# A head's values at a pitch of 80 columns instead of 65 in a chunked attention and feed-forward kernel

## The chip, the cores and the metric

The kernel runs on one core of one Trainium2 chip. The core has five engines that run their own instruction streams: TensorE (PE, matrix multiplications, with weight loads beside it: PEld), VectorE (DVE), ScalarE (ACT), GpSimd (POOL) and SyncE (SP). Sixteen DMA engines move data between the device's memory and the on-chip memory; here GpSimd issues every load that casts from 32-bit to 16-bit floats (queue q0, software_dynamic) and SyncE issues all others (queue q1, hardware_dynamic). The metric is the device time of one execution in microseconds (us), the median of five runs.

## The reference

Four batches, eight heads, 768 positions, 64 values to a head. Positions are cut into chunks of 32. A chunk attends to eight memory keys of its head and to the keys from 16 positions ahead of the chunk to 8 behind it. The heads' outputs, side by side (512 wide), go through a layer norm and a feed-forward of width 2048 with a residual:

```
for each chunk c:
    k_full = concat(mem_k, k[l_start:r_end]);  v_full = concat(mem_v, v[l_start:r_end])
    a      = softmax(q[chunk] @ k_full.T / 8)
    x[chunk] = a @ v_full
xn  = (x - mean(x)) / sqrt(var(x) + 1e-6) * g_ln
out = x + relu(xn @ w_ch1) @ w_ch2
```

All inputs and the output are 32-bit floats; the kernel multiplies in 16-bit.

## The kernel before, in words

A *tile* is 128 positions; there are 24, six to a batch. A *unit* is three tiles, and the main loop at the end of the kernel walks over eight units. In unit u TensorE does the feed-forward of that unit's three tiles: sixteen steps of `up` (each 128 of the 2048 hidden columns, L319, followed by a ReLU on VectorE for even steps, L327, on ScalarE for odd ones, L325), then twelve steps of `down` (L336). Between the steps a plan written by hand places the attention work of the next unit's tiles: `scores` (L238), exponentials on ScalarE (L245), `values` (L258), `norm` on VectorE (L268 to L278), `turn_x` (L296), and the preparation of keys and queries for a later batch (`kq_block`: turns on TensorE at L176, copies on VectorE at L191 and on ScalarE at L201). The order of each engine's work is the order in which the program is written; each engine waits only for the data and buffers that it needs. Two pairs of PSUM buffers (`att`) serve attention and the turns, four single ones (`mm`) the feed-forward.

Weights for the whole feed-forward stay on chip (`w1c0` to `w1c3`, `w2c0` to `w2c3`). They are loaded once, by GpSimd, in the same queue as the first batch's keys, queries and values. In the order of issue: four loads of keys and queries, value groups 0 to 3, groups 4 and 5, `w1c0` to `w1c2`, the rest of keys and queries, `w1c3`, `w2c0`, `w2c1`, value groups 6 and 7, `w2c2`, groups 8 to 11, `w2c3`. Eight semaphores go round for these loads, so the ninth load after another is issued only when that one has landed.

Before the loop, a start is written out by hand: turns of the first keys and queries, `scores` and `values` of tiles 0 to 2, with multiplications of a zero tile between them (`stay_busy`, L310) that only keep TensorE occupied. `values` of tile t needs the value groups 2t and 2t+1.

The buffer that the change touches is `V` (two of them, one to a batch in turn): 128 rows, then 12 groups of 64 positions, then 8 heads, then `HD` columns of 16-bit floats. Rows 0 to 7 hold the memory values, rows 8 to 95 the positions around a group. Of a head's columns the first 64 are the values and the next one is 1.0, so that the matmul at L258 gives the sum of the exponentials as its 65th column. Who writes `V`:

- `clear_v` (L376 to L386, VectorE): zeros in the rows that fall outside the sequence (L378, L379), ones in column 64 of groups 1 to 10 (L380), and a copy of a 0/1 column into column 64 of groups 0 and 11 (L383). It is called once in the start for `V0` and once in unit 0, at step 8, for `V1`.
- `load_v_group` (L114): one group, up to 88 rows by 8 heads, 64 values each. Batches 0 and 1 are loaded so.
- `load_v_head` (L120): one head, 64 rows by 12 groups. Batches 2 and 3 are loaded so, and `v_around` (L128, L129, SyncE) then copies the overlapping rows from group to group.
- `v_mem` (L133, SyncE): the memory values, from `memv16`, which has the same columns.

Of the kernel before, what the change touches and what calls it, by code (L numbers as in the profile page):

```python
# [15 lines left out]
def kernel(  # L16
# [12 lines left out]
    nc = tc.nc  # L29
# [3 lines left out]
    NG = 12  # L33
    KR = 96
    KC = NG * KR + 32
    HD = 65
    CUT = 64

    ctx.enter_context(tc.manual_schedule())
# [5 lines left out]
    memk16 = sb.tile([128, 2, 64], FP16, name="memk16")  # L45
    memv16 = sb.tile([72, B, H, HD], FP16, name="memv16")[64:72, :, :, :]
    memv32 = sb.tile([72, 512], FP32, name="memv32")[64:72, :]
# [12 lines left out]
    q16 = [sb.tile([96, H, 8, 64], FP16, name=f"q16_{i}") for i in range(2)]  # L60
    V = [sb.tile([128, NG, H, HD], FP16, name=f"V{i}") for i in range(2)]
    KT = [sb.tile([128, 4, KC], FP16, name=f"KT{i}") for i in range(2)]
# [19 lines left out]
    def slot(kind):  # L82
        lst = {"att": att, "mm": mm}[kind]
        turn[kind] = (turn[kind] + 1) % len(lst)
        return lst[turn[kind]]

    def dram(t, offset, pattern):
        return bass.AP(tensor=t.tensor, offset=offset, ap=[list(p) for p in pattern])

    def free(ap, off, pattern, parts=None):  # L90

        p = list(ap.ap[0]) if parts is None else [ap.ap[0][0], parts]
        return bass.AP(tensor=ap.tensor, offset=ap.offset + off, ap=[p] + [list(x) for x in pattern])
# [37 lines left out]
    def v_mem(b):  # L131
# [3 lines left out]
            in_=bass.AP(tensor=src.tensor, offset=src.offset,  # L135
                        ap=[list(src.ap[0]), [0, NG], [1, H * HD]]),
        )
# [115 lines left out]
    def values(b, t):  # L253
        p = summed[t] = slot("att")
        for h in range(H):
            for gg in range(2):
                c0 = 128 * (h % 4)
                nc.tensor.matmul(  # L258
                    out=p[64 * gg : 64 * gg + 64, h // 4, c0 : c0 + HD],
                    lhsT=AT[t % 3][0:KR, gg, h, :],  # L260
                    rhs=V[b % 2][0:KR, 2 * t + gg, h, :],
                    start=(h % 4 == 0), stop=(h % 4 == 3), tile_position=(0, 64 * gg),
                )

# [111 lines left out]
    def clear_v(i, between=lambda: None):  # L376

        nc.vector.memset(V[i][0:32, 0, :, 0:64], 0.0)  # L378
        nc.vector.memset(V[i][64:96, NG - 1, :, 0:64], 0.0)  # L379
        nc.vector.memset(V[i][:, 1 : NG - 1, :, 64:65], 1.0)  # L380
        between()
        for c, g in enumerate((0, NG - 1)):
            nc.vector.tensor_copy(  # L383
                out=free(V[i][:, g, 0, 64:65], 0, [[HD, H]]),
                in_=free(counts[:, c : c + 1], 0, [[0, H]]),
            )  # L386
# [10 lines left out]
    nc.vector.memset(busy, 0.0)  # L397
    nc.vector.memset(counts, 1.0)
    nc.vector.memset(ones32, 1.0)
    nc.vector.memset(memv16[:, :, :, 64:65], 1.0)  # L400
    nc.sync.dma_start(out=memk32, in_=dram(mem_k, 0, [[64, 128], [128 * 64, 2], [1, 64]]))
    nc.sync.dma_start(out=g_one, in_=dram(moe_g_ln, 0, [[0, 1], [1, 512]]))
    nc.sync.dma_start(out=memv32, in_=dram(mem_v, 0, [[64, 8], [512, H], [1, 64]]))
# [7 lines left out]
    nc.scalar.copy(out=memv16[:, 0, :, 0:64], in_=memv32.rearrange("p (h d) -> p h d", h=H))  # L411
    stay_busy(10)
    clear_v(0, lambda: clear_q(0, 0))
    clear_q(0, 1)
    clear_k(0)
# [28 lines left out]
    for g in range(8, NG):  # L444
# [3 lines left out]
        out=memv16[:, 1:B, :, 0:64],  # L448
# [31 lines left out]
    scores(0, 1)  # L480
    stay_busy(5)
    values(0, 0)
    norm(0, 0)
    scores(0, 2)
    stay_busy(1)
    values(0, 1)
    norm(1, 1)
    stay_busy(4)
    values(0, 2)
    norm(2, 2)  # L490
    stay_busy(2)
# [11 lines left out]
    for u, tiles in enumerate(units):  # L503
# [18 lines left out]
        if u == 0:  # L522
            at(1, clear_q, 1, 0)
            at(5, clear_q, 1, 1)
            at(8, clear_v, 1)
            at(11, clear_k, 1)
            for j in (0, 2):
# [19 lines left out]
        elif u in (2, 4):  # L547
            attend(((1, 8, 8, 12), (4, 8, 10, 14), (11, 17, 17, 21)))
            b = u // 2 + 1
# [13 lines left out]
        for step in range(16 + 4 * n):  # L563
            if step < 16:
                up(u, n, step)
            else:
                i, part = divmod(step - 16, 4)
                if u == 0:
                    d = step - 16
                    i, part = divmod(d, 2) if d < 6 else (d % 3, d // 3)  # L570
# [36 lines left out]
```

The softmax here doesn't subtract the row's maximum and nothing guards it: scores larger than these inputs give would overflow.

## Time and profile before

| what | value |
|---|---|
| median of five runs | 232.03 us (231.02 to 233.15) |
| the profiled execution: its time, its span | 231.44 us, 229.7 us |
| PE busy | 222.7 us (97%) |
| DVE, ACT, POOL busy | 125.5 us (55%), 119.0 us (52%), 68.5 us (30%) |
| DMA queue q0 (GpSimd's loads) | 45680 packets, 14.23 MB |
| DMA queue q1 (SyncE's) | 4602 packets, 7.33 MB |
| value loads, `load_v_group` | 24, of which 20 with 88 KB each, 13.2 us from issue to landing (median) |
| value loads, `load_v_head` | 16, 96 KB each, 5.4 us |
| granted TensorE clock | 9 tenths or more in every slice |

Busy time is the sum over an engine's instructions; the KB of a load are those that it writes. A DMA share over 1 in a window means that more packets are under way on the sixteen engines than one each. The GB/s of a window count the bytes as written: a load that casts reads twice as many.

### The profile page before, as it was taken

How to read it: one execution, taken by the hardware profiler on the slowest of the kernel's cores; microseconds unless marked ns; L12 is line 12 of the kernel's file. 1: busy time of each engine (PE TensorE's matmuls, PEld its weight loads, DVE VectorE, ACT ScalarE, POOL GpSimd, SP SyncE). 2: the span in 40 equal slices, each digit the busy share in tenths (PEclk: the TensorE clock that was granted, in tenths of full speed). 3: DMA queues.
4: the chain of work that ended last, by engine and by line, in shares of the span. 5: the costliest groups of instructions: out<-in, count | busy, mean ns of one | idle time of the engine just before them, and what ended most of it. 6: DMA issues, size and time to landing. Idle time of an engine off the chain costs nothing.

```text
span 229.7 us, 5499 instructions
## 1 busy us (share of the span) xinstructions
PE 222.7 (97%) x2289; PEld 138.3 (60%) x2289; DVE 125.5 (55%) x290; ACT 119.0 (52%) x228; POOL 68.5 (30%) x125
## 2 busy tenths in 40 slices
PE   7988999999999999999999999999999999999993
PEld 2554676547765577555765577556764576556553
DVE  5756781565737638575436548674436542663222
ACT  3674648353893576655356367654456345534200
POOL 6974344677360370540001360410001200030000
PEclk9999999999999999999999999999999999999999
DMA  5999999999999999548921199553001200111012
GB/s 76 176 88 202 205 211 152 143 202 229 105 74 157 202 135 29 37 85 122 236 38 49 60 115 24 37 101 104 0 3 46 91 3 0 47 49 46 0 49 93
DMA packets 50307, 21.91 MB, mean 95 GB/s; under 512 B 37817, under 2 KB 46777, under 8 KB 50234
## 3 DMA queue, kind: packets, MB, share of 16 engines
q0 software_dynamic: 45680, 14.23, 89.1%
q1 hardware_dynamic: 4602, 7.33, 10.5%
q8 instruction: 18, 0.29, 0.6%
q14 instruction: 7, 0.06, 0.1%
HBM read 28.48 MB, written 6.29 MB: 151 GB/s over the span
## 4 chain that ended last, share of the span: by engine, by line
PE 77%; DMA 16%; POOL 2%; DVE 2%; issue 1%; POOLq 0%
PE mm L319 32%; PE mm L336 32%; DMA w2c<-in_moe_w_ch_dram 13%; PE att L238 4%; DMA V<-in_v_dram 4%; PE att L258 3%; PE att L176 3%; PE att L296 2%; PE mm L354 2%; POOL V L114 1%; PE mm L176 1%; DVE QZ L374 1%; POOL w2c L146 0%; DVE V L379 0%; DVE V L378 0%
## 5 line engine op out<-in xcount | busy, mean ns | idle before, releaser
L319 PE MATMUL mm<-xT,w1c 128*128 128x384 f16 x512 | 88.3, 327 | 0.0
L336 PE MATMUL mm<-w2c,rT 128*128 128x512 f16 x368 | 87.4, 380 | 0.6 <-DMA w2c<-in_moe_w_ch_dram 0.6
L319 PEld LDWEIGHTS <-w1c 128*128 128x128 f16 x512 | 57.0, 114 | 24.2 <-issue 0.3
L327 DVE TENSOR_SCALAR rT<-mm 128x384 f16<-128x384 f32 x64 | 35.5, 557 | 35.5 <-PE mm L319 35.4
L336 PEld LDWEIGHTS <-rT 128*128 128x128 f16 x368 | 33.8, 98 | 34.4 <-issue 0.7
L325 ACT ACTIVATE rT<-mm 128x384 f16<-128x384 f32 x64 | 31.2, 489 | 35.9 <-PE mm L319 33.9
L245 ACT ACTIVATE AT<-att,band 96x512 f16<-96x512 f32 x48 | 30.1, 677 | 17.1 <-PE att L238 16.6
L287 POOL TENSOR_SCALAR veps<-squares 128x1 f32<-128x1 f32 x24 | 4.5, 188 | 110.3 <-ACT junk L284 95.5
L343 DVE SCALAR_TENSOR_TENSOR osb<-mm,rstd,xs 128x512 f32<-128x512 f32 x23 | 17.2, 750 | 31.3 <-PE mm L336 20.8
L114 POOL DMA_DIRECT2D V<-in_v_dram x24 | 21.4, 897 | 15.2 <-DMA w1c<-in_moe_w_ch_dram 3.7
L301 ACT COPY xT<-att 128x512 f16<-128x512 f16 x21 | 12.2, 581 | 23.3 <-PE att L296 23.3
L191 DVE COPY KT<-att 128x80 f16<-128x80 f16 (+3 forms) x44 | 18.4, 481 | 2.1 <-PE att L176 2.1
L278 DVE SCALAR_TENSOR_TENSOR xn<-xs,nmean,g_row 128x512 f16<-128x512 f32 x24 | 18.0, 752 | 0.9
L201 ACT COPY QZ<-mm 64x768 f16<-64x768 f16 (+1 forms) x18 | 13.6, 757 | 7.4 <-PE mm L176 7.2
L284 ACT ACTIVATE junk<-xs,nmean 128x512 f16<-128x512 f32 x24 | 17.4, 724 | 0.1
L268 DVE RECIPROCAL rec<-att 128x8 f32<-128x8 f32 x24 | 4.9, 203 | 22.9 <-PE att L258 22.9
L269 DVE SCALAR_TENSOR_TENSOR xs<-att,rec 128x512 f32<-128x512 f32 x24 | 16.6, 691 | 0.8
L238 PE MATMUL att<-QZ,KT 128*128 128x128 f16 x192 | 14.8, 219 | 0.7 <-ACT AT L245 0.5
L238 PEld LDWEIGHTS <-KT 128*128 128x128 f16 x192 | 12.6, 98 | 4.3 <-issue 1.2
L201 ACT COPY QZ<-att 64x384 f16<-64x384 f16 (+1 forms) x20 | 12.0, 598 | 5.3 <-PE att L176 5.1
L291 POOL TENSOR_TENSOR rstd<-veps,mhalf 128x1 f32<-128x1 f32 x24 | 13.3, 553 | 2.0
L258 PEld LDWEIGHTS <-AT 96*64 96x64 f16 x384 | 8.1, 111 | 8.7 <-issue 5.5
(63 smaller groups left out, 145.4 us busy)
## 6 DMA issues: line engine op xcount, KB each, us to landing
out_dram<-osb SPq DMA_DIRECT2D x23, 256.0 KB, 5.7
w1c<-in_moe_w_ch_dram POOLq DMA_DIRECT2D x4, 512.0 KB, 11.8
w2c<-in_moe_w_ch_dram POOLq DMA_DIRECT2D x4, 512.0 KB, 15.0
V<-in_v_dram POOLq DMA_DIRECT2D x20, 88.0 KB, 13.2
k<-in_k_dram POOLq DMA_DIRECT2D x2, 768.0 KB, 12.3
q<-in_q_dram POOLq DMA_DIRECT2D x2, 768.0 KB, 15.5
V<-in_v_dram POOLq DMA_DIRECT2D x16, 96.0 KB, 5.4
k<-in_k_dram POOLq DMA_DIRECT2D x3, 256.0 KB, 5.9
```

Of the source, the lines that this page charges most:

```text
L114: nc.gpsimd.dma_start(out=V[b % 2][r : r + hi - lo, g, :, 0:64], in_=dram(v, b * H * HS + lo * D, [[64, hi - lo], [HS, H], [1, 64]]),)
L191: copy(out=free(KT[b % 2], j * KC + 24 + 32 * ga + 8 * lo, [[KR, gb - ga], [8, m], [1, 8]]), in_=free(pv, lo, [[8, gb - ga], [1, m], [n, 8]]),
L201: copy(out=free(QZ[b % 2][rows, j, g0, par, :], 0, [[128, g1 - g0], [8, 8], [1, 8]]), in_=free(pv[rows, :], 8 * g0, [[8, g1 - g0], [1, 8], ...
L238: nc.tensor.matmul(out=p[:, gg, 128 * j : 128 * j + 128], lhsT=KT[b % 2][:, j, KR * g : KR * g + 128], rhs=QZ[b % 2][:, j, g, :, :], start ...
L245: nc.scalar.activation(out=free(a, 32 * c, [[512, 2], [64, 8], [1, 32]], KR), in_=free(p, 32 * c, [[512, 2], [64, 8], [1, 32]], KR), func= ...
L278: nc.vector.scalar_tensor_tensor(out=xn[i], in0=x, scalar=nmean[i], in1=g_row, op0=ALU.add, op1=ALU.mult,)
L284: nc.scalar.activation(out=junk, in_=xs[xi], func=ACTF.Square, bias=nmean[i], accum_out=squares[i],)
L319: nc.tensor.matmul(out=p, lhsT=free(w, i, [[4, 128]]), rhs=xT[u % 2][:, dt, 0 : 128 * n], start=(dt == 0), stop=(dt == 3),)
L325: nc.scalar.activation(out=o, in_=p, func=ACTF.Relu)
L327: nc.vector.tensor_scalar(out=o, in0=p, scalar1=0.0, scalar2=None, op0=ALU.max)
L336: nc.tensor.matmul(out=p, lhsT=rT[hc][:, 128 * i : 128 * i + 128], rhs=w2c[hc // 4][:, hc % 4, :], start=(hc == 0), stop=(hc == 15),)
L343: nc.vector.scalar_tensor_tensor(out=o, in0=p, scalar=rstd[t % 9], in1=xs[t % 9], op0=ALU.mult, op1=ALU.add,)
```

## The change

`HD` becomes 80. A head's columns now take 160 bytes instead of 130, so every head's values begin at a multiple of 32 bytes. The spare columns 65 to 79 hold ones as well: `clear_v` writes columns 64 to 79 of all twelve groups in one memset, ahead of the copy at L383 that sets column 64 of groups 0 and 11, and the memset of `memv16` (L400) does the same. The multiplication at L258 still takes 65 columns.

```diff
-    HD = 65
+    HD = 80
...
-                    out=p[64 * gg : 64 * gg + 64, h // 4, c0 : c0 + HD],
+                    out=p[64 * gg : 64 * gg + 64, h // 4, c0 : c0 + 65],
                     lhsT=AT[t % 3][0:KR, gg, h, :],
-                    rhs=V[b % 2][0:KR, 2 * t + gg, h, :],
+                    rhs=V[b % 2][0:KR, 2 * t + gg, h, 0:65],
...
         nc.vector.memset(V[i][0:32, 0, :, 0:64], 0.0)
         nc.vector.memset(V[i][64:96, NG - 1, :, 0:64], 0.0)
-        nc.vector.memset(V[i][:, 1 : NG - 1, :, 64:65], 1.0)
+        nc.vector.memset(V[i][:, :, :, 64:HD], 1.0)
...
-    nc.vector.memset(memv16[:, :, :, 64:65], 1.0)
+    nc.vector.memset(memv16[:, :, :, 64:HD], 1.0)
```

The copies at L128, L129 and L133 and the strided copy at L383 are written in terms of `HD` and follow it: a memory row of one group is 1280 bytes instead of 1040, and a row of eleven groups 14080 bytes instead of 11440. The number of instructions on every engine, their order and the number of DMAs stay.

## The prediction

> **What bounds the kernel now.** I read the page first: TensorE is busy 97% of the span, at full clock. So an edit that lightens a DMA or VectorE is worth only the moments at which TensorE stands still for it. I then took the table of waits, TensorE's rows only, and the timeline around them.
>
> ```profile
> PE 222.7 (97%) x2289; PEld 138.3 (60%) x2289; DVE 125.5 (55%) x290; ACT 119.0 (52%) x228; POOL 68.5 (30%) x125
> ...
> PE mm L336 <- DMA w2c<-in_moe_w_ch_dram: 0.6, 1, 0.6
> ...
> PE att L258 <- DMA V<-in_v_dram: 0.8, 2, 0.5
> ```
>
> ```profile
> 14.47 0.65 PE L258 MATMUL att<-V,AT 96*64 96x65 f16 x16
> 16.32 0.59 PE L258 MATMUL att<-V,AT 96*64 96x65 f16 x16
> 16.84 1.04 PE L310 MATMUL mm<-busy 128*128 128x512 f16 x4
> 18.18 0.19 PE L258 MATMUL att<-V,AT 96*64 96x65 f16 x1 [0.30 <-DMA V<-in_v_dram]
> 18.88 0.42 PE L258 MATMUL att<-V,AT 96*64 96x65 f16 x15 [0.51 <-DMA V<-in_v_dram]
> ...
> 48.50 1.89 PE L336 MATMUL mm<-w2c,rT 128*128 128x512 f16 x8 [0.55 <-DMA w2c<-in_moe_w_ch_dram]
> ```
>
> Columns are start, length, engine, line. Sixteen of the L258 matmuls take 0.38 us elsewhere in the chain. Here the first two groups of sixteen take 0.65 and 0.59, and the third runs from 17.8 (when its exponentials are ready) to 19.30. All three wait inside for value groups: by the trace's landings groups 1, 3 and 5 land at 14.7, 16.5 and 18.8. Later TensorE waits once for a load, 0.55 us for `w2c3` at 48.5. After that it waits for no load at all. So everything the change can gain through its loads lies before 49 us, and it is about 1.7 us.
>
> **How fast the value loads go.** Windows of the trace (us, TensorE, PEld, DVE, ACT, POOL busy, clock, DMA share, GB/s written):
>
> ```profile
> 10.00:12.00 2.00, 2.00 (x40) 1.06 (x39) 1.10 (x3) 1.72 (x5) 2.00 (x3) 1.00 3.82 107
> 12.00:16.00 4.00, 3.34 (x46) 2.25 (x45) 1.32 (x4) 2.51 (x5) 2.94 (x5) 1.00 4.00 79
> 20.00:24.00 4.00, 3.97 (x29) 2.25 (x26) 1.65 (x5) 3.07 (x6) 1.55 (x2) 1.00 1.25 207
> 86.00:89.00 3.00, 3.00 (x48) 2.30 (x41) 2.86 (x9) 0.98 (x3) 0.00 (x0) 1.00 4.51 59
> ```
>
> Weights (20 to 24) go at 207 GB/s; values (12 to 16) at 79, with three times the packets under way; at 86 to 89 values alone go at 59. The packet records say how: of the 28,992 packets of 128 bytes, 17,807 take 30 to 35 ns, and the rest lie mostly between 60 and 300. The short time shows no charge for a crooked address: from the packets of 1024 bytes (98 ns) and 4096 (324 ns) a straight line gives 23 ns plus 73.5 ns per 1024 written, and so 32 ns at 128. But the slow packets come in a body, after 1 to 2.5 us of dense loads (from 10.3 us on, and from 84.3 on), and isolated loads of one head (94.5 to 97 us) hardly have them. That looks like writes that are accepted at once and then pile up. Of what, the trace does not tell: partly written words, reads in 256-byte pieces, or sheer number.
>
> **Rule against row.** The Trainium skill, page "DMA: Bandwidth & Descriptors", section Specifications, says that below 512 bytes a transfer is not at line rate because the DMA engine reads, modifies and writes. A run of values stays 128 bytes, so by the rule the loads stay slow at either pitch, and the gain is nothing. The rows agree that small runs are slow (79 against 207 GB/s) but do not say that alignment is without effect. At 130 bytes a 128-byte run touches 4.94 words of 32 bytes on average (counted over 12 groups and 8 heads; 6 of 96 runs are aligned), at 160 bytes exactly 4, all whole. By count of words alone the value phase shortens by 19%; if partly written words cost more, by more. The floor is 0%. I take 19% or more, because the packets under way show pressure on writing, and because little is needed: the last landing must come only 1 us earlier out of the 8.4 us from the landing of the last queries ahead of them (10.4) to 18.8 (12%).
>
> **Part 1, loads of values in the start.** With group 1 landed in time the first `values` ends 0.27 us sooner (0.65 against 0.38); the third would run 17.8 to 18.2 instead of ending at 19.30, where exponentials and not the loads end the wait. That is 1.1 us, and the 0.27 lies inside it. Later loads queue behind the values in the same queue, so `w2c3` comes at least 1 us earlier too; its wait of 0.55 us goes. The `w1c` loads had landed before their steps, so nothing else becomes late. Sum: -1.65.
>
> **Part 2, VectorE in the start.** Prices come from rows of memsets:
>
> ```profile
> L374 DVE MEMSET QZ<- 64x1536 uint32 x4 | 5.4, 1338 | 1.2 <-issue 1.2
> L378 DVE MEMSET V<- 32x512 f16 x2 | 1.0, 485 | 0.2
> L397 DVE MEMSET busy<- 128x256 uint32 x1 | 0.3, 272 | 0.9 <-PEq L591 0.9
> L380 DVE MEMSET V<- 128x80 f16 x2 | 0.2, 125 | 0.3 <-issue 0.3
> L400 DVE MEMSET memv<- 8x32 f16 x1 | 0.1, 85 | 0.2 <-issue 0.2
> ```
>
> A memset costs 58 ns plus 0.833 ns per element, whatever its type. L380 grows from 80 to 1536 elements: 125 to 1338 ns. L400 grows from 32 to 512: 85 to 485. L378 and L379 become writes of 256 words of four bytes in the built program instead of 512 halves: 485 to 272 each. Ahead of the copy L383 VectorE is later by 0.40 - 0.43 + 1.21 = 1.19 us. Two things queue behind L383: SyncE's `v_mem` (issued at 5.38) and GpSimd's first value load (issued at 5.51, after 0.59 us of waiting for exactly this). Both start 1.19 later, and so do the five value loads and three `w1c` issues after them. What hides it: packets of keys and queries occupy the DMA engines until 9.6, and packets of values begin at 8.7; with the first load issued at 6.70 they still can. Groups 4 and 5 are issued at 11.2 and 12.1 instead of 10.0 and 10.9; the shortest landing of an unhindered value load is 3.0 us (`load_v_head`), so they can land by 15.1 and are not needed before 17.8. VectorE's own queue: its copies of keys (7.46 to 9.06) end at 10.25, the next had been waiting for TensorE until 9.67, the one after until 11.40, so 0.6 + 0.9 us of waiting absorb 1.19. TensorE rewrites those buffers at 10.66. Cost 0; uncovered it would be 1.19.
>
> **Part 3, the second `clear_v`, step 8 of unit 0.** It costs 1.21 - 0.43 = 0.79 us more on VectorE, between two ReLUs. Its key copies (L191) now end near 33.5 instead of 32.69:
>
> ```profile
> 31.43 1.49 PE L319 MATMUL mm<-xT,w1c 128*128 128x384 f16 x8
> ...
> 32.10 0.59 DVE L191 COPY KT<-att 128x352 f16<-128x352 f16 x2
> 32.84 0.87 PE L176 MATMUL att<-identity,k 96*64 96x96 f16 x32
> ...
> 33.88 0.87 PE L176 MATMUL att<-identity,q 96*64 96x96 f16 x32 [0.17 <-ACT QZ L201]
> ```
>
> The turn at 32.84 reuses the buffer that these copies empty, so TensorE would wait until 33.5 or so; of that, 0.17 was to be waited before the next turn anyway. Cost 0.5 us (between 0.3 and 0.65). The next ReLU on VectorE had 1.21 us of waiting ahead of it.
>
> **Part 4, the rest.** `v_around` and `v_mem` carry 23% more bytes. Packets of 11440 bytes take at most 1.6 us and end near 108; the batch's values are multiplied at 119. Cost 0, and with that cover gone under 1 us. The L258 matmuls move 65 columns from another pitch: 32 in 0.65 against 16 in 0.38 is 17 ns each, and 65 columns at L336's pace (512 in 216 ns) are 27 ns, two at a time 13.7. At best 3.3 ns x 384 = 1.3 us gained, at worst as much lost if a stride matters; I take 0, since nothing in the rows tells the pitch.
>
> **Sum.** -1.65 + 0.5 = -1.15 us on the profiled execution's 231.44 (span 229.7 and 1.7 around it): 230.3. The median of the runs is 0.6 higher; against it 232.03 - 1.15 = **230.9 us**.
>
> **The rivals.**
> - *The loads don't drain faster* (0.30). For it: the flat 32 ns and the rule. Then the landings stay, since the queue and not the issue sets them; the 0.5 us of part 3 arrives at `w2c3`, where 0.55 us were to be waited anyway. 0 to +0.5: 232.2.
> - *Slower: the longer memset reaches TensorE* (0.08). If the value loads had been issue-bound after all, all landings come 1.19 later, `w2c3` as well, and part 3 adds its 0.65: +1.8, 233.8. It decides as soon as group 5 lands later than 18.8. Against it: group 5 now lands 7 us after its issue ended, which is queueing.
> - *More than the waits* (0.07). The L258 matmuls gain their 1.3 us too: 229.6.
>
> **How the numbers follow.** The forecast has 0.55, with 230.2 to 231.6 as its own range. A measurement of this kernel can tell about 1% (2.3 us) from no change. Below 229.7 come most of the last case and a tail of the first: 0.12. Above 234.35 comes a tail of the slower case and of the spread of runs: 0.06. The range takes in the second case with the runs' spread and most of the fourth: 229.5 to 233.2.
>
> **What would show it.** Right: value windows at 10 to 16 us above 100 GB/s written, group 5 landed before 17.8, no TensorE wait for `V` or `w2c`, L380 at 1.34 us, a new wait of 0.3 to 0.8 us for VectorE at L176 near 32. Wrong: value windows as before (first rival), or L258 still waiting at 18 or later.

## The result, and the profile after

The changed kernel takes 231.68 us (median of 43 runs, 229.95 to 233.76) against 231.88 us for the kernel before in the same comparison (80 runs); the ratio is 0.9969, with a 95% interval of 0.9953 to 0.9985, or 0.7 us. This ratio is one of means, and it leaves out every run that took over 1.5% more than the fastest of its own kernel: eight of the changed kernel's (233.41 us and more), but none of before's, of which 21 took 232.9 us or more. With all runs the means differ by 0.3 us (231.73 against 232.02; resampling these runs gives an estimated 95% interval from 0.7 faster to 0.1 slower). So the time lies on the side that was forecast and within the range, but the gain is less than the 1.15 us of the sum, and over all executions it cannot be told from none. Which executions gain and which do not, the last section shows.

The page and the windows of the changed kernel answer to those of before (in the windows: the stretch, then busy time of PE, PEld, DVE, ACT and POOL, granted clock, DMA share, GB/s written):

```profile
PE 223.3 (97%) x2289; PEld 137.8 (60%) x2289; DVE 127.4 (55%) x290; ACT 119.0 (52%) x228; POOL 68.8 (30%) x125
...
q0 software_dynamic: 45680, 14.23, 57.2%
```

```profile
10.00:12.00 2.00, 2.00 (x5) 0.51 (x5) 0.94 (x3) 0.93 (x3) 2.00 (x3) 0.50 2.13 165
12.00:16.00 4.00, 3.79 (x58) 2.28 (x57) 1.17 (x3) 2.31 (x5) 2.90 (x6) 0.97 2.63 122
86.00:89.00 3.00, 3.00 (x53) 2.35 (x53) 2.82 (x8) 0.71 (x2) 0.00 (x0) 1.00 0.79 54
```

The loads got faster. Queue q0 moves the same 45680 packets and 14.23 MB, but their time falls from 89.1% to 57.2% of the engines' span. The value loads' windows write 165 and 122 GB/s where they wrote 107 and 79. The 28,992 packets of 128 bytes take 35.0 ns on average instead of 72.7; 97% now take the undisturbed 32 ns or so, before it was 61%. At 86 to 89 us the DMA share is 0.79 instead of 4.51, because the six loads of heads issued from 80 us on have landed by 87.8 us instead of 91.2. Group 5, the last that the start needs, lands at 16.8 us instead of 18.8.

TensorE's rows, the one wait that is new, and VectorE's memsets:

```profile
16.00 0.44 PE L258 MATMUL att<-V,AT 96*64 96x65 f16 x16
17.85 0.44 PE L258 MATMUL att<-V,AT 96*64 96x65 f16 x16
19.19 0.44 PE L258 MATMUL att<-V,AT 96*64 96x65 f16 x16
23.25 7.31 PE L319 MATMUL mm<-xT,w1c 128*128 128x384 f16 x44
...
34.36 0.87 PE L176 MATMUL att<-identity,k 96*64 96x96 f16 x32 [0.89 <-DVE KT L191]
...
48.81 1.89 PE L336 MATMUL mm<-w2c,rT 128*128 128x512 f16 x8
```

```profile
L380 DVE MEMSET V<- 128x1536 f16 x2 | 2.7, 1338 | 0.8 <-issue 0.8
L378 DVE MEMSET V<- 32x256 uint32 x2 | 0.5, 272 | 0.1
L400 DVE MEMSET memv<- 8x512 f16 x1 | 0.5, 485 | 0.2 <-issue 0.2
```

All waits for `V` and for `w2c3` are gone (each sixteen at L258 runs in 0.44 us; none is named as waiting). In their place stands 0.89 us for VectorE at 34.36. Yet this execution is not shorter: span 229.9 against 229.7. One thing has to be known to read it. The windows show a granted clock of 0.50 at 10 to 12 us: for 3.4 us, from 8.8 to 12.2, TensorE had half its speed. The profiled execution of before had no such stretch. The stretch comes in some executions of either kernel and not in others, and the last section comes back to it. It also means that this trace alone does not show the loads to be what ended the waits: TensorE came to the first `values` 1.5 us later than before (16.00 instead of 14.47). Experiment 4 has traces without the stretch.

### The profile page after: what moved, and what is told of

Read it like the earlier page. It is cut to its first block, busy times and chain, and to the rows that moved or that the text cites. A ratio compares the mean times of both kernels' runs of the same rounds, so it can differ in the third digit from the quotient of the medians.

```text
span 229.9 us, 5500 instructions
## 1 busy us (share of the span) xinstructions
PE 223.3 (97%) x2289; PEld 137.8 (60%) x2289; DVE 127.4 (55%) x290; ACT 119.0 (52%) x228; POOL 68.8 (30%) x125
## 3 DMA queue, kind: packets, MB, share of 16 engines
q0 software_dynamic: 45680, 14.23, 57.2%
## 4 chain that ended last, share of the span: by engine, by line
PE 88%; DVE 6%; DMA 2%; issue 2%; POOL 0%; DVEq 0%; POOLq 0%
PE mm L336 35%; PE mm L319 33%; PE att L238 5%; PE att L176 4%; PE att L258 3%; DMA q<-in_q_dram 2%; PE att L296 2%; PE mm L176 2%; PE mm L354 2%; PE att L310 1%; DVE rT L327 1%; DVE xs L269 1%; PE mm L310 1%; DVE xn L278 1%; DVE QZ L374 1%
## 5 line engine op out<-in xcount | busy, mean ns | idle before, releaser
L114 POOL DMA_DIRECT2D V<-in_v_dram x24 | 21.5, 902 | 9.5 <-DMA w1c<-in_moe_w_ch_dram 4.3
L301 ACT COPY xT<-att 128x512 f16<-128x512 f16 x21 | 12.2, 581 | 22.4 <-PE att L296 22.4
L191 DVE COPY KT<-att 128x80 f16<-128x80 f16 (+3 forms) x44 | 18.4, 483 | 2.4 <-PE att L176 2.4
L284 ACT ACTIVATE junk<-xs,nmean 128x512 f16<-128x512 f32 x24 | 17.4, 724 | 0.1
L120 POOL DMA_DIRECT2D V<-in_v_dram x16 | 12.2, 768 | 0.3 <-issue 0.3
## 6 DMA issues: line engine op xcount, KB each, us to landing
w2c<-in_moe_w_ch_dram POOLq DMA_DIRECT2D x4, 512.0 KB, 14.5
q<-in_q_dram POOLq DMA_DIRECT2D x2, 768.0 KB, 14.5
```

Source lines behind the costliest of these rows:

```text
L114: nc.gpsimd.dma_start(out=V[b % 2][r : r + hi - lo, g, :, 0:64], in_=dram(v, b * H * HS + lo * D, [[64, hi - lo], [HS, H], [1, 64]]),)
L191: copy(out=free(KT[b % 2], j * KC + 24 + 32 * ga + 8 * lo, [[KR, gb - ga], [8, m], [1, 8]]), in_=free(pv, lo, [[8, gb - ga], [1, m], [n, 8]]),
L284: nc.scalar.activation(out=junk, in_=xs[xi], func=ACTF.Square, bias=nmean[i], accum_out=squares[i],)
```

## Experiments

**1. The pitch without the alignment.** Pitch 80 as in the change, but the values start at a column `C0` that is not 0.

```diff
-            out=V[b % 2][r : r + hi - lo, g, :, 0:64],
+            out=V[b % 2][r : r + hi - lo, g, :, C0 : C0 + 64],
...
-                    rhs=V[b % 2][0:KR, 2 * t + gg, h, 0:65],
+                    rhs=V[b % 2][0:KR, 2 * t + gg, h, C0 : C0 + 65],
```

In `shift1` the start is 1, so every head lies 2 bytes off:

> Pitch 80 as in the change, but the values sit in columns 1 to 64 and the ones in 65, so every head begins 2 bytes past a 32-byte boundary. The memsets of ones are as in the change (L380 1.34 us), one small memset for column 0 more. If partly written words are what slows the loads (theory): packets pile up as before, windows 12 to 16 us near 80 GB/s written, value group 5 lands near 19 us, L258 waits for V again, and the time is that of before or up to 0.5 us above it. If the pitch of 160 bytes does it (rival: another spread over banks): as in the change, queue q0 near 57% of the engines' span, group 5 landed by 15.7, time 0.7 us under before.

The ratio was 1.0303 (1.0265 to 1.0342), much slower than before; the expectation of "up to 0.5 us above" was too mild. A line of its page (packets, MB, share of the engines' span), one of its waits (us in total, times, longest) and one of its DMA issues (times, KB each, median us to landing):

```profile
q0 software_dynamic: 45680, 14.23, 115.5%
```

```profile
PE att L259 <- DMA V<-in_v_dram: 4.1, 5, 1.3
```

```profile
V<-in_v_dram POOLq DMA_DIRECT2D x16, 96.0 KB, 8.0
```

So the pitch is not what helps. With pitch 80 and crooked starts the packets of 128 bytes average 110 ns, worse than before's 72.7, the loads of heads land in 8.0 us instead of 5.4, and TensorE waits for `V` in the start and again near 50 us (`values` is L259 in this kernel, one line having been added). Not all of the time lost is the loads': this execution also had half speed for 6.8 us in the start and 3.4 us from 52 us on, and 1.8 us of waiting for L191's counterpart.

In `shift8` the start is 8, or 16 bytes off:

> The same with values in columns 8 to 71, 16 bytes past a 32-byte boundary. If the word is 32 bytes: slow loads as in shift1. If the word is 16 bytes: fast loads as in the change. If pitch alone counts: fast as well. Only together with shift1 does it tell the size of the word.

The packets average 42.9 ns and the loads of heads land in 3.3 us, as in the change. The loads are fast although no head lies on a 32-byte boundary. The ratio was 1.0048 (1.0026 to 1.0069), slower all the same: this kernel has one more memset of 768 elements (0.70 us) in each `clear_v`, and TensorE's wait for L191's counterpart grew to 1.69 us.

**2. How large is the word?** One number of the two runs pointed to a smaller one. In the kernel before heads lie 130 bytes apart, so the four odd heads begin 2 bytes off a 4-byte boundary and the four even ones on one. Its 72.7 ns lie halfway between the 35.0 of the change and the 110.3 of `shift1`, where all eight are off. `shift2` starts at column 2, or 4 bytes off:

> The change's pitch of 80 with values in columns 2 to 65, 4 bytes past a 32-byte boundary. Theory A: packets as in shift8 (about 43 ns), far from the 110 ns of shift1; time near shift8's, 1.1 us above before at most, because of its longer memsets. Theory B or 16-byte words: packets as in shift1, 100 ns or more, ratio 1.03.

It averages 36.2 ns, with q0 at 57.7%, and the ratio is 1.0011 (0.9985 to 1.0036): the loads are fast, but this kernel too has the longer memsets, and its wait for L191's counterpart is 1.1 us. So a start on 4 bytes is as good as one on 32 (36.2 against 35.0), and one 2 bytes past a 4-byte boundary is what costs. Then a pitch of 66 columns must do, with two columns of ones instead of sixteen:

```diff
-    HD = 80
+    HD = 66
```

> HD = 66: heads 132 bytes apart, every head on a 4-byte but not on a 32-byte boundary; the ones take columns 64 and 65 (192 elements, 0.22 us instead of 1.34). Theory A (what costs is a 4-byte word written in part, as the odd heads of the kernel before and all heads of shift1 do): packets of 128 bytes average 35 to 45 ns, value group 5 lands by 16.5 us, no wait for V or w2c and none for L191 near 34; 1.4 us under before, so ratio 0.994, as good as the change with clear_v moved. Theory B (32-byte words): packets average 70 ns or more, group 5 near 19 us, ratio 1.0.

The ratio was 0.9930 (0.9907 to 0.9954), lower than that of the change; over all of its executions the mean is 1.0 us under before's. A line of its page, and its memsets (busy us, mean ns of one, idle before):

```profile
q0 software_dynamic: 45680, 14.23, 63.1%
```

```profile
L378 DVE MEMSET V<- 32x256 uint32 x2 | 0.5, 272 | 0.1
L380 DVE MEMSET V<- 128x192 f16 x2 | 0.4, 218 | 0.2
```

Packets average 41.7 ns. TensorE waits for neither `w2c` nor L191, and the third `values` runs its 0.45 unhindered (here too TensorE had a stretch at half speed, and came to it at 19.19 us). `pitch72` stands between, with heads on 16-byte boundaries and ones of 768 elements:

> HD = 72: 144 bytes, heads on 16-byte boundaries, every other one on a 32-byte boundary; ones 768 elements, 0.70 us. Theory A: as pitch66 in the loads (35 to 45 ns), and a stall at L191 of about half the change's, ratio 0.995. Theory B with 32-byte words: half the heads slow, packets near 55 ns, q0 near 73%.

Packets average 37.5 ns and the ratio is 0.9944 (0.9914 to 0.9974); over all executions its mean is only 0.4 us under before's, which cannot be told from none: nine of the 22 are listed like those in which TensorE is slow until 13 us (last section). The stall of about half the change's was a miss: no wait for L191 is named in its waits.

**3. What the longer memsets cost.** `late` is the change, with the second `clear_v` moved to where VectorE idles:

```diff
-            at(8, clear_v, 1)
+            at(16, clear_v, 1)
...
-                at(15, load_v_group, 1, g)
+                at(17, load_v_group, 1, g)
```

> The change, with clear_v of V1 moved from step 8 to step 16 of unit 0 (VectorE idles there for 4.9 us in the changed kernel) and the six value loads that depend on it from step 15 to 17. Theory: the new 0.89 us wait of TensorE for L191 near 34 us goes, of which about 0.6 was not there before; the time falls by 0.6 us against the change, 1.3 us under before. Rival: something else takes the wait's place at once (the ScalarE copies of L201 that ended the earlier wait): at most 0.2 us.

The ratio was 0.9933 (0.9909 to 0.9958), and over all executions the mean is 1.0 us under before's. The wait of 0.89 us is gone and the 0.18 us for ScalarE is back in its place, as before the change:

```profile
36.18 0.87 PE L176 MATMUL att<-identity,q 96*64 96x96 f16 x32 [0.18 <-ACT QZ L201]
36.98 2.14 PE L319 MATMUL mm<-xT,w1c 128*128 128x384 f16 x12
```

So the memset at step 8 alone takes back 0.6 us, by the timeline (below). The two ratios put it at 0.0036 of the time, or 0.8 us, but they come from two comparisons, so that difference is known only to about 0.7 us. Laid side by side by the listed clock (last section), the change takes 0.5 to 0.8 us longer than the kernels without the stall. `slowset` is the converse, the kernel before with VectorE's extra time and nothing else:

```diff
         nc.vector.memset(V[i][:, 1 : NG - 1, :, 64:65], 1.0)
+        nc.vector.memset(spare_cols[:, 0:880], 1.0)
...
     nc.vector.memset(memv16[:, :, :, 64:65], 1.0)
+    nc.vector.memset(spare_cols[:, 0:410], 1.0)
```

> The kernel before (pitch 65, slow loads) with the change's extra VectorE time alone: a memset of a spare tile of 880 columns in clear_v (0.79 us) and one of 410 in the start (0.40 us). Theory: the start hides its part and the wait for w2c3 at 48.5 us hides the stall at L176, so 0 to +0.5 us against before. Rival: the start's 1.2 us reach the value loads and the end: +1.2 us or more.

The ratio was 1.0008 (0.9985 to 1.0030), no difference beyond 0.7 us, although the same stall shows in its trace (L259 and L192 are L258 and L191 there):

```profile
16.78 0.46 PE L259 MATMUL att<-V,AT 96*64 96x65 f16 x16
...
35.12 0.87 PE L177 MATMUL att<-identity,k 96*64 96x96 f16 x32 [0.86 <-DVE KT L192]
```

This execution had TensorE at half speed from 7.7 to 14.5 us, so it waits for neither `V` nor `w2c3`, and the trace does not show that a wait swallows the stall. The times by listed clock speak for it in one kind of execution: at 1.000 and under 232.7 us, `slowset` has a median of 231.60 (7) and before 231.67 (34), no difference. Between 0.990 and 0.994 it is 232.37 (5) against 231.64 (35), at 0.982 to 0.985 232.72 (6) against 232.22 (18). So the prediction's statement that before, the wait for `w2c3` swallowed such a delay fits where TensorE has full clock from about 6 us on; in the other two groups the stall costs 0.5 to 0.7 us, and in this trace the wait is not there.

The traces settle a rival as well. In the change, `pitch66`, `pitch72` and `thin2` the first value load is issued at 4.86 us instead of 5.51, and an earlier issue could be what brings the values sooner. In `slowset` it is issued at 6.84, 1.33 us later than before, and group 5 still lands at 18.6 us instead of 18.8; in `shift8` it is issued at 5.45, as before, and group 5 lands at 17.4. So a later issue did not move the landing, and faster packets moved it without an earlier issue.

**4. All of the alignment, none of the stall.** `thin2` sets only column 64 in `clear_v` and fills the spare columns of both buffers while VectorE idles:

```diff
-        nc.vector.memset(V[i][:, :, :, 64:HD], 1.0)
+        nc.vector.memset(V[i][:, 1 : NG - 1, :, 64:65], 1.0)
...
+            at(16, fill_memv)
+            at(17, fill_spare, 0)
+            at(18, fill_spare, 1)
```

> The change's pitch and full alignment, with VectorE's extra time taken out of both busy places: only column 64 is set in clear_v (125 ns, as before), and the spare columns of both buffers are filled at steps 17 and 18 of unit 0, where VectorE idles. Theory: no stall at L191; 1.5 us under before, ratio 0.9935, the same as late and, if theory A holds, as pitch66. If the whole 32 bytes bring more than 4-byte boundaries do (rival), thin2 is faster than pitch66 by 0.3 us or more.

The ratio was 0.9936 (0.9912 to 0.9960); over all executions the mean is 1.2 us under before's. `late`, `pitch66` and `thin2` are the same within their intervals (about 0.55 us either way), so full alignment brings nothing beyond what 4 bytes bring that these runs could tell. All three have a lower ratio than the change; `pitch66` does it with one number changed and was not timed against the change directly, only through the kernel before.

The profiled executions of `thin2` and of `pitch72` had full clock throughout from 5.4 and 6.2 us on, as that of before had from 6.0. So their rows can be laid beside before's. Of `thin2`:

```profile
14.29 0.44 PE L258 MATMUL att<-V,AT 96*64 96x65 f16 x16
16.14 0.44 PE L258 MATMUL att<-V,AT 96*64 96x65 f16 x16
17.48 0.44 PE L258 MATMUL att<-V,AT 96*64 96x65 f16 x16
...
21.54 7.31 PE L319 MATMUL mm<-xT,w1c 128*128 128x384 f16 x44
...
49.31 4.06 PE L319 MATMUL mm<-xT,w1c 128*128 128x384 f16 x24
```

Of `pitch72`:

```profile
14.58 0.44 PE L258 MATMUL att<-V,AT 96*64 96x65 f16 x16
...
21.83 7.31 PE L319 MATMUL mm<-xT,w1c 128*128 128x384 f16 x44
```

In `thin2` the feed-forward starts at 21.54 instead of 22.70, the second unit's at 49.31 instead of 51.31, and the span is 227.6 instead of 229.7. Of the 1.16 us in the start, 0.18 were there before the first `values` (14.29 instead of 14.47), because full clock came 0.6 us sooner; the loads bring the other 0.98. `pitch72` says the same: it comes to the first `values` 0.11 us later than before and to the feed-forward 0.87 sooner, which makes 0.98. Another 0.84 come by the end of unit 0, and nothing after that.

## Why the prediction was right, point by point

- **TensorE is the bound, and only its waits before 49 us are to be had.** Right: after 51 us next to nothing was gained in the two traces that can be compared (`thin2`: 2.0 us ahead at 49.31, 2.1 at the end; `pitch72`: 1.7 at 49.61, 1.8 at the end).
- **Rule against row.** The page's rule for small transfers would have left the loads as slow as they were. The runs of 128 bytes stay under 512 in all kernels, and their mean time went from 36.2 to 110.3 ns (`shift2`, `shift1`) with nothing but a start 2 bytes earlier at the same pitch. The choice for the row was right. Its reason was wrong in the size: starts on whole words matter, but the word is 4 bytes and not 32. The count of 4.94 against 4.00 words, which gave 19%, measures nothing real: `shift1` and `shift2` both touch five 32-byte words in every run and differ by a factor of three. The phase from the landing of the last queries to that of group 5 did shorten by about as much (8.4 us before, 6.7 in the change, 6.6 in `pitch72`, 6.3 in `thin2`: 20 to 25%); that 19% came so near is luck.
- **Part 1, -1.65 us.** The start was put at -1.1 and the loads' part of it measured -0.98. The wait for `w2c3` was put at -0.55; the stretch to the second unit's start shrank by 0.84. Of this, 0.11 are a half-wait inside L258 near 46 us (0.55 instead of 0.44), and 0.72 are the wait for `w2c3`: from the start of `turn_x` to that of the next `down` take 0.94 us before (47.56 to 48.50) and 0.22 in `thin2` (46.28 to 46.50), because without the wait the two overlap by 0.17. So the loads brought 1.8 us here. Two readings of the prediction were off without effect on its sum: it set the 0.65 us of the timeline beside 0.38 from the chain, where the timeline itself has 0.45 for an unhindered sixteen (41.10 us), so the first `values` had 0.2 to gain and not 0.27; and the straight line through its packets rises by 75.3 ns and not 73.5 per 1024 bytes, which leaves 32 ns at 128. The ratios say -1.5 to -1.6 us for the three kernels without the stall, all their executions -1.0 to -1.2, for the reason given under the clock below.
- **Part 2, VectorE in the start, 0.** The prices held to the nanosecond (1338, 272, 485). Right in effect, wrong in one detail: the value loads did not start 1.19 us later but 0.65 us *earlier* (at 4.86 instead of 5.51). In the built program of before the first value load had waited for the copy at L383; here, and in `thin2` with its short memset, it no longer does. Why is not shown. That a delay of the issue costs nothing here was right for the reason given: `slowset` issues 1.33 us later than before and lands no later.
- **Part 3, the stall, +0.5.** The step was right in place and cause, and a little too small. In the timeline TensorE needs 3.86 us from the `up` steps at 31.98 to those at 35.84, where it needed 3.26, so 0.6, within the range given for it. L383, L380 and the ReLU had overlapped in before's records at 30.7 to 31.5; the longer memset does not overlap, and the key copies end at 34.3 after a start of the unit that was 0.55 late, or 1.06 later than before relative to it, where 0.8 was reckoned.
- **The sum.** -1.15 was forecast and -0.3 to -0.7 measured. The mechanism held term by term where TensorE has full clock from about 6 us on, and there the change is 0.7 us ahead. What the prediction had not seen is that in other executions TensorE comes late to the start and the waits that the loads end are shorter or absent, while the stall remains. That the total lies in the range is in part luck: the range was wide and holds the time of the kernel before as well.
- **The rivals.** That the loads don't drain faster fell: 57.2% against 89.1%. That the longer memset delays all landings (233.8) fell with `slowset`, whose group 5 lands no later, and with the result. That the L258 matmuls themselves gain from the pitch fell: sixteen run in 0.44 or 0.45 us at pitches 66, 72 and 80, and in 0.45 at pitch 65 where they don't wait (41.10 us).

## What to carry to other kernels

If a load casts to 16 bits and writes many short runs, give every run a start on a multiple of 4 bytes, with one spare element to the row; more padding brought nothing here. What fills the padding is paid on an engine, so pad by the least that does it, and fill it where that engine idles: sixteen columns instead of two cost 0.6 us, about half of the gain at full clock and all of it otherwise. In a kernel that is bound by one engine, count the gain of a faster load as that engine's waits, look at what these waits had been hiding, and ask whether the waits are there in every execution.

## What the runs showed of the hardware

**Odd starts.** 128-byte runs written by the casting loads, by the start of a head: all on 4 bytes or better 34.1 to 42.9 ns a packet (seven kernels, starts on 4 to 32 bytes), half of them 2 bytes off 69.0 and 72.7 ns (two kernels), all of them 2 bytes off 110.3 ns (one). More than half of the packets take 32 ns in every one of them; what differs is how many pile up behind others. The reads are the same in all these kernels, so the cost lies in the write. What the write does with an odd start is not shown.

**The clock in the start.** Executions of one kernel fall into groups, and each group has a trace on record. In all of them TensorE runs at half speed at first: ten matmuls of `stay_busy` take 4.45 us from 1.24 on in the kernel before, and five take 1.25 us at 9.48. The record of the granted clock begins where full speed is first reached, and the 1.00 that the views print before that is no reading. In `before`, `pitch72` and `thin2` full speed comes at 5.4 to 6.2 us and stays. In the change and in `pitch66` a stretch of 3.41 us at half speed follows within the start, in `slowset` one of 6.83. In `late` and `shift2` full speed comes only at 13.4 and 13.8 us. The same turn of keys, before and in `late`:

```profile
8.86 0.69 PE L176 MATMUL mm<-identity,k 64*64 64x64 f16 x32
```

```profile
11.11 1.06 PE L176 MATMUL mm<-identity,k 64*64 64x64 f16 x32
```

Medians in us by the mean clock listed for an execution, with the number of executions (before's are those of the comparisons in the experiments; a listed 1.000 has two sorts, with none between 232.5 and 232.7 us):

| listed clock | half speed in the traces | before | the change | `late`, `pitch66`, `thin2` |
|---|---|---|---|---|
| 0.995 to 0.999 | until 5.4 us (`thin2`) | 231.05 (14) | 230.31 (13) | 229.72 (12) |
| 1.000, under 232.7 us | until 6.0 (`before`), 6.2 (`pitch72`) | 231.67 (34) | 230.47 (1) | 229.63 (14) |
| 0.990 to 0.994 | and 3.4 us more (the change, `pitch66`) | 231.64 (35) | 231.67 (16) | 230.90 (21) |
| 0.982 to 0.985 | and 6.8 us more (`slowset`) | 232.22 (18) | 232.50 (6) | 232.02 (7) |
| 1.000, over 232.7 us | until 13.4 us (`late`) | 233.06 (25) | 233.53 (8) | 232.94 (12) |

The longer TensorE is slow in the start, the less the fast loads bring: 1.3 us in the first row (`late`, `pitch66`, `thin2` against before), 2.0 in the second, then 0.7, 0.2 and 0.1. At full speed the kernel before waits for values in the start, and a slow TensorE arrives in time for them: in `slowset` the three `values` run in 0.46 us or less with the slow loads. The stall is paid in every row, so the change is 0.7 us ahead in the first, level in the third, and 0.3 and 0.5 behind in the last two. The second row agrees, on a single execution of the change. Why an execution falls into one group and not another was not tried. The Trainium skill, page "TensorE: Matmul & The Clock Gate", section "Part 1: The HAM clock gate", says that activity is judged in free-running windows of 3.4 us; the length agrees with the stretch in the changed kernel's record (3.41 us) and with twice that in `slowset`, and no run here tests the rest.
